# Clustered attention and a gated MLP: key tiles in float32, a pair taken head by head, and a new order of work

## The chip, the cores and the metric

The kernel runs on one core of one Trainium2 chip. The core has five engines that run side by side, each through its own queue in order: TensorE (PE) multiplies matrices, VectorE (DVE), ScalarE (ACT) and GpSimd (POOL) work on tiles, and SyncE (SP) issues transfers. The metric is the device time of one execution in microseconds; less is better.

## The reference

Four batches, eight heads, 768 positions, 64 columns a head, 16 clusters. Everything is float32. Cut to what is computed:

```python
# attention, for each batch and head
q_assign = argmax(normalized(q) @ normalized(centroids).T)
k_assign = argmax(normalized(k) @ normalized(centroids).T)
scores = where(q_assign[:, None] == k_assign[None, :], q @ k.T / 8, -1e9)
attn = softmax(scores)
out = attn @ v
# the heads side by side give x: [4, 768, 512]
h = relu(x @ w_in)                 # [4, 768, 1024]
u, v = h[..., :512], h[..., 512:]
v_n = (v - mean(v)) / sqrt(var(v) + 1e-6)
v_s = einsum('ts,bsd->btd', w_spatial, v_n) + b_spatial[None, :, None]
result = (u * v_s) @ w_out
```

## The kernel before

The kernel works on pairs of heads: four pairs make a batch, sixteen the whole. Products that must keep float32 accuracy are made of float16 parts: a tile is written as a high part (a cast on ACT) and a low part (what the cast left over), and three products of parts are summed in PSUM. A row of the profile names the tile without its number.

A pair goes through three functions. `prep(n)` loads k and q (`raw`) and v (`vraw`), makes high parts (`hq`, L616) and low parts (`lo`, L622 on DVE, or L619 and L620 on ACT and POOL for the pairs in `LO_POOL`), multiplies with the centroids (L638 to L640), finds each position's cluster by five DVE operations (L651 to L656) and puts the one-hot rows into `hq` (L686 for pair 0, transposing transfers for the others). It also makes the parts of v (`vhl`, L690 and L695, or L692 and L693 for the pairs in `VL_POOL`) and v's sums over all keys (by PE for the pairs in `SUM_PE`, L703 and L704; else by a DVE reduction, L711, and one small float32 product, L712). `shifts(n)` finds each query's largest score: products L754 on PE, maxima L761 on DVE (18 instructions a pair, over 24 products), and brings the result as extra rows into `hq` (L774 to L793). `attend(n)` makes the scores (L823 and L825: 24 products of 512 columns and 24 of 256 a pair), the exponentials on ACT (L830, 18 a pair, into the float32 tiles `p`), and for each of 12 key tiles a pair (six a head) a cast on ACT (L842), a subtraction on POOL (L846) and 18 products with the values on PE (L852: for each of six query blocks high by high, high by low, low by high, each with 65 or 64 moving columns; 228 a pair with those that add the mean).

`mlp(b)` follows a batch, in groups of six products of 512 columns (all at L900): first v (with mean and variance on DVE, L928 and L929, a chain of small operations for the inverse root, L934 to L939, of which the power, L935, is on POOL, and the normalization L941 on DVE), then u, the product with w_spatial (L900 `vn`, `wsp`) with the gating L964 to L966, a transposing transfer (`gT`), and the product with w_out.

The order of the instructions is made by a planner in the kernel: every operation has a cost, a due time and a key, and whenever an engine comes free in the plan's own time, the ready operation with the least due time plus key is written next on it. Engines then run their queues in that order. Attention and MLP work are interleaved on PE in this way, so that the MLP's long products fill in where a pair's scores or values are not ready.

Of the kernel before, what the change touches and what calls it, by code (L numbers as in the profile page):

```python
# [7 lines left out]
F32 = mybir.dt.float32  # L8
# [69 lines left out]
KC = -44.31  # L78
# [45 lines left out]
SHIFT = {}  # L124
# [66 lines left out]
class Plan:  # L191


    def __init__(self):
        self.ops = []
        self.rings = []
        self.due = None
        self.tag = ""
# [6 lines left out]
    def op(self, eng, cost, fn, after=(), use=(), new=(), claim=(), key=0.0, at=0.0, dma=None, turn=False, cols=0, alt=None, due=None, port=None):  # L205
# [4 lines left out]
        o.key = key + SHIFT.get(o.tag, 0.0) if key < FILLER else key  # L210
        o.eng, o.cost, o.fn, o.key, o.at, o.dma, o.turn, o.cols, o.alt = eng, cost, fn, key, at, dma, turn, cols, alt
# [127 lines left out]
def kernel(  # L339
# [43 lines left out]
    ohx = const.tile([P, NT, 8, C], F16, name="ohx")  # L383
    shx = [const.tile([P, NT, P], F16, name="shx%d" % i) for i in range(1)]
# [17 lines left out]
    held = {"wou": wou}  # L402

# [36 lines left out]
    r_vhl = R(None, "vhl", None, None, V_BUFS, tiles=vhl)  # L440
    scratch = r_p32.new()
# [15 lines left out]

    ld_c = op("SP", 0.6, lambda: nc.sync.dma_start(out=cn(0), in_=cent), new=[scratch], dma=0.1, key=KC)
    ld_i = op("SP", 0.6, lambda: nc.sync.dma_start(out=idt(), in_=ident), use=[scratch], dma=0.2, key=KC)
# [7 lines left out]
    c_wt = op("DVE", 1.2, fill, key=-8)  # L467
    c_id = op("DVE", 0.2, lambda: V.tensor_copy(out=id16, in_=idt()), after=[ld_i], use=[scratch], key=0)
    c_z = op("DVE", 0.5, lambda: (V.memset(cmh, 0.0), V.memset(cml, 0.0)), key=-8)
    c_oh = op("POOL", 1.0, lambda: (G_.memset(ohx, 0.0), G_.memset(ohx.rearrange("p t (x e) c -> p t x (e c)", e=2)[:, :, 0:2, C:C + 1], PEN)), key=-8)  # L470
    c_sh = op("POOL", 2.0, lambda: [G_.memset(x, 0.0) for x in shx], key=-7)
    c_mean = op("POOL", 0.6, lambda: [G_.memset(x, 0.0) for x in mean], key=-6)
    c_wh = op("POOL", 0.5, lambda: (G_.memset(one32, 1.0), [G_.memset(x[:, :, D:D + 1], S * MEAN_UNIT) for x in whs], [G_.memset(x[:, :, D:D + 1], 0.0) for x in wls]), key=-5)
    c_one = op("POOL", 0.8, lambda: [G_.memset(x[:, :, :, D:D + 1], 1.0) for x in vhl], key=-9)
# [11 lines left out]
        (0.25, lambda: V.tensor_scalar(out=cn(0), in0=cn(0), scalar1=ninv, scalar2=C_SCALE, op0=ALU.mult, op1=ALU.mult)),  # L486
        (0.22, lambda: V.tensor_copy(out=cn(1), in_=cn(0))),
# [560 lines left out]
```

## Time and profile before

| what | us |
|---|---|
| median of three runs | 665.71 |
| lowest, highest | 665.3, 668.3 |
| span of the profiled execution | 666.4 |

The profiled execution's own time is not listed apart from the three; its span lies among them, 0.7 us above the median. Busy time is an engine's share of the span in which at least one of its instructions ran. A matmul's duration on PE holds its way through the array, which the next matmul overlaps: the pace is read from start to start, not from the duration. Idle time of an engine costs something only where another engine waits for it.

### The profile page before, as it was taken

To read this page: it belongs to the slowest core of one execution; us is meant where nothing else is said; L and a number is where in the kernel's file an instruction comes from. 1 tells how busy PE (TensorE), PEld (TensorE's weight loads), DVE (VectorE), ACT (ScalarE), POOL (GpSimd) and SP (SyncE) were. 2 spreads that over 40 slices of the span, in tenths; PEclk is the share of its full clock that TensorE was granted. 3 is DMA by queue.
4 is the path that set the end of the run, shared out by engine and by line. 5 is a ranking of instruction groups with operands and counts; after the bars stand their busy time and mean duration, and the time that the engine had idled before them with its cause. 6 is when DMAs were issued, how large, how long until landed. Compare 5 with 4: busy or idle time off the path is not lost.

```text
span 666.4 us, 16687 instructions
## 1 busy us (share of the span) xinstructions
PE 624.9 (94%) x6757; PEld 374.9 (56%) x6757; DVE 446.3 (67%) x828; ACT 454.6 (68%) x875; POOL 426.5 (64%) x305
## 2 busy tenths in 40 slices
PE   1799988889999999989999999999999999999996
PEld 1466665556556665656666465566665564444442
DVE  5899989999999979966969756764378210142100
ACT  6489998998879796869876596259984761232211
POOL 3268997988877886677796486149996681132210
PEclk9999998999999999989999999999999999999999
DMA  5656876684733785787434616133023203220124
GB/s 171 156 118 137 174 168 176 153 194 74 161 97 73 165 169 157 168 157 164 133 73 92 157 44 135 35 83 60 9 59 53 60 10 56 54 64 32 32 63 95
DMA packets 105939, 70.49 MB, mean 106 GB/s; under 512 B 90315, under 2 KB 93062, under 8 KB 105862
## 3 DMA queue, kind: packets, MB, share of 16 engines
q1 hardware_dynamic: 102118, 62.74, 43.1%
q10 hardware_dynamic: 3744, 6.69, 2.8%
q8 instruction: 53, 0.87, 0.5%
q14 instruction: 24, 0.20, 0.1%
HBM read 27.63 MB, written 6.29 MB: 51 GB/s over the span
## 4 chain that ended last, share of the span: by engine, by line
PE 66%; DVE 16%; DMA 8%; ACT 7%; issue 2%; SPq 0%; POOL 0%; POOLq 0%; DVEq 0%; ACTq 0%
PE acc L900 36%; PE acc L852 11%; PE acc L823 6%; PE acc L825 6%; DVE nm L761 6%; PE acc L754 5%; DMA gT<-ghl 2%; ACT pt L842 2%; ACT p L830 2%; DVE lo L622 2%; DMA vraw<-in_vp_dram 1%; DMA raw<-in_kqT_dram 1%; DMA wraw<-in_wsT_dram 1%; DMA sht<-shx 1%; DMA hq<-sht 1%
## 5 line engine op out<-in xcount | busy, mean ns | idle before, releaser
L846 POOL TENSOR_TENSOR pt<-p,pt 128x768 f16<-128x768 f32 x192 | 319.9, 1692 | 60.6 <-ACT pt L842 39.9
L761 DVE TENSOR_REDUCE nm<-acc 128x1 f32<-128x512 f32 (+1 forms) x288 | 185.6, 678 | 28.8 <-PE acc L754 27.4
L830 ACT ACTIVATE p<-acc 128x512 f32<-128x512 f32 x288 | 156.3, 598 | 25.0 <-PE acc L825 20.8
L842 ACT CAST pt<-p 128x768 f16<-128x768 f32 x192 | 152.2, 835 | 2.0
L852 PEld LDWEIGHTS <-pt 128*128 128x128 f16 x3456 | 129.0, 98 | 33.2 <-POOL pt L846 4.4
L852 PE MATMUL acc<-vhl,pt 128*128 128x65 f16 (+1 forms) x3456 | 138.4, 193 | 3.1 <-POOL pt L846 2.8
L900 PE MATMUL acc<-win,xT 128*128 128x512 f16 x576 | 137.9, 379 | 0.2
L823 PE MATMUL acc<-hq,lo 128*128 128x256 f16 (+1 forms) x384 | 111.0, 330 | 5.4 <-ACT p L830 4.5
L825 PE MATMUL acc<-hq 81*128 81x256 f16 (+1 forms) x384 | 111.2, 330 | 1.8 <-DMA hq<-sht 1.7
L900 PE MATMUL acc<-vn,wsp 128*128 128x512 f16 x432 | 102.1, 379 | 0.0
L754 PE MATMUL acc<-hq 80*128 80x256 f16 (+1 forms) x384 | 92.9, 339 | 3.8 <-DVE nm L761 1.5
L966 POOL TENSOR_TENSOR ghl<-u,ghl 128x512 f16<-128x512 f32 x24 | 28.5, 1188 | 100.6 <-ACT ghl L965 89.1
L900 PEld LDWEIGHTS <-xT 128*128 128x128 f16 x576 | 55.3, 97 | 62.4 <-issue 2.1
L964 DVE SCALAR_TENSOR_TENSOR u<-acc,bsp,u 128x512 f32<-128x512 f32 x24 | 18.0, 749 | 84.6 <-PE acc L900 84.5
L900 PE MATMUL acc<-wou,gT 128*128 128x512 f16 x288 | 70.1, 383 | 2.3 <-DMA gT<-ghl 2.3
L900 PEld LDWEIGHTS <-wsp 128*128 128x128 f16 x432 | 41.4, 97 | 45.8 <-issue 0.2
L965 ACT CAST ghl<-u 128x512 f16<-128x512 f32 x24 | 14.8, 617 | 61.5 <-DMA gT<-ghl 36.2
L823 PEld LDWEIGHTS <-lo 128*128 128x128 f16 x384 | 35.6, 98 | 31.5 <-issue 9.0
L754 PEld LDWEIGHTS <-hq 80*128 80x128 f16 x384 | 34.9, 100 | 24.9 <-issue 4.5
L825 PEld LDWEIGHTS <-hq 81*128 81x128 f16 x384 | 37.8, 98 | 18.0 <-issue 6.3
L900 PEld LDWEIGHTS <-gT 128*128 128x128 f16 x288 | 28.1, 98 | 34.7 <-DMA gT<-ghl 3.0
L943 POOL TENSOR_TENSOR vn<-v,vn 128x512 f16<-128x512 f32 x24 | 28.8, 1219 | 19.3 <-ACT vn L942 19.3
(108 smaller groups left out, 642.7 us busy)
## 6 DMA issues: line engine op xcount, KB each, us to landing
raw<-in_kqT_dram SPq DMA_DIRECT2D x15, 768.0 KB
vraw<-in_vp_dram SPq DMA_DIRECT2D x16, 384.0 KB
out_dram<-o ACTq DMA_DIRECT2D x24, 256.0 KB
hq<-hq SPq DMA_DIRECT2D x15, 384.0 KB
vn<-in_w_in_dram SPq DMA_DIRECT2D x8, 512.0 KB
hq<-lo SPq DMA_DIRECT2D x16, 192.0 KB
lo<-hq SPq DMA_DIRECT2D x16, 192.0 KB
wraw<-in_wsT_dram SPq DMA_DIRECT2D x12, 192.0 KB
```

The lines of the kernel that those rows point to most:

```text
L754: T.matmul(out=acc.t[:, c:c + cs.stop - cs.start], lhsT=hq.t[0:R_SH, 1, h, t * P:(t + 1) * P], rhs=hq.t[0:R_SH, 0, h, cs], start=c == 0, s ...
L761: V.tensor_reduce(out=nm.t[:, t, k:k + 1] if n == 1 else nm.t[:, t:t + n, k], in_=src, axis=AX.X, op=ALU.max, negate=True)
L823: T.matmul(out=o, lhsT=lo.t[:, h, ks], rhs=hq.t[:, 2, h, cs], start=x == 0, stop=False, skip_group_check=True)
L825: T.matmul(out=o, lhsT=hq.t[0:R_E, 0, h, ks], rhs=hq.t[0:R_E, 1, h, cs], start=False, stop=True, skip_group_check=True)
L830: o = op("ACT", 0.6, lambda: A.activation(out=p32.t[:, j0:j0 + n_, cs], in_=sc.t.rearrange("p (t c) -> p t c", t=n_), func=AF.Exp, bias=P_ ...
L842: o = op("ACT", 0.83, lambda pt=pt, p32t=p32t: A.copy(out=pt.t[:, 0, :], in_=p32t()), after=[done[k % 2], done[2]], use=[p32], new=[pt], k ...
L846: los_.append(op("POOL", 1.64 if SPLIT == 1 else 0.09 + 1.64 / SPLIT, lambda pt=pt, p32t=p32t, qs=qs: G_.tensor_tensor(out=pt.t[:, 1, qs], ...
L852: T.matmul(out=av.t[:, t * (D + 1):t * (D + 1) + w], lhsT=lhsT, rhs=rhs, skip_group_check=True, **f)
L900: T.matmul(out=acc.t, lhsT=lr[m][0], rhs=lr[m][1], start=(m == 0), stop=(m == n - 1))
L943: l = op("POOL", 1.16, lambda t=t, v=v: G_.tensor_tensor(out=vn[:, 1, t, :], in0=v.t, in1=vn[:, 0, t, :], op=ALU.subtract), after=[h], use ...
L964: o = op("DVE", 0.75, lambda: V.scalar_tensor_tensor(out=u32.t, in0=acc.t, scalar=bsp[:, t:t + 1], in1=u32.t, op0=ALU.add, op1=ALU.mult), ...
L966: l = op("POOL", 1.16, lambda: G_.tensor_tensor(out=ghl.t[:, 1, :], in0=u32.t, in1=ghl.t[:, 0, :], op=ALU.subtract), after=[h], use=[u32, ...
```

## The change

- **Key tiles in float32.** In the four pairs of the first batch, two of six key tiles of each head (`WHOLE`, tiles 1 and 4) no longer get a cast and a subtraction. Their exponentials meet the values as float32: six products a tile of 65 columns in place of 18 float16 ones. The float32 values (`vf`) lie in the space of the weight tile `wou`, whose loads therefore wait until the last such product; an ACT operation writes them.
- **Low parts moved to GpSimd.** `LO_POOL` takes pairs 2 and 3 as well, `VL_POOL` pairs 2, 3 and 4. The sums of v of pairs 4 to 7 go from DVE to PE.
- **Pair 0 head by head.** `prep0` makes high parts, logits, clusters, one-hot rows and their transposes for one head and then the other, in pieces; the centroids' parts are written by ACT and DVE; `shifts(0)` brings head 0's result in two parts (four key tiles, then two).
- **The inverse root in the MLP.** Its small operations move from DVE to POOL, and in batch 0 ACT normalizes in place of DVE.
- **Order from a table.** `STARTS` holds a rank for each operation; the rank takes the place of due time and key.

```diff
+WHOLE = {0: [(0, 1), (0, 4), (1, 1), (1, 4)], 1: [(0, 1), (0, 4), (1, 1), (1, 4)], 2: [(0, 1), (0, 4), (1, 1), (1, 4)], 3: [(0, 1), (0, 4), (1, 1), (1, 4)]}
-LO_POOL = (1,)
-VL_POOL = (0, 1)
-SUM_PE = tuple(range(4))
+LO_POOL = (1, 2, 3)
+VL_POOL = (0, 1, 2, 3, 4)
+SUM_PE = (0, 1, 2, 3, 4, 5, 6, 7)
+C_TINY = 0.25
+NORM_ACT = (0,)
...
+        if self.starts is not None and key < FILLER:
+            o.due, o.key = float(self.starts[len(self.ops)]), 0.0
...
+    wouf = wou.rearrange("p a t f -> p (a t f)").bitcast(F32)
+    vw = NT * 2 * (D + 2)
+    vfs = [wouf[:, vw * i:vw * (i + 1)].rearrange("p (t h d) -> p t h d", h=2, d=D + 2) for i in range(VF_BUFS)] if WHOLE else []
...
+            o = o_vs = op("ACT", 0.83, lambda: A.activation(out=full(), in_=vraw.t.rearrange("p t (h d) -> p t h d", d=D), func=AF.Copy, scale=V_SCALE), after=[o_vh, c_one], use=[vraw], new=[vf] if vf else [], key=KV)
+            if n in VL_POOL:
+                o_vl = op("POOL", 1.59, lambda: G_.tensor_tensor(out=vh.t[:, :, :, D + 2:], in0=full(), in1=vh.t[:, :, :, 0:D], op=ALU.subtract), after=[o], use=[vf or vraw, vh], key=KV)
...
+    def prep0():
...
+        for h in range(2):
+            kh = h * K0_HEAD
...
+            lg = op("PE", 0.35, logits, at=A0_H1 * h, after=[hi, low] + c_cm, use=[hq, lo], new=[misc], cols=576, key=K0_LG + kh)
...
+            o = op("DVE", 0.35, lambda lgf=lgf, mx=mx: V.tensor_reduce(out=mx.t[:, 0:NA], in_=lgf(), axis=AX.X, op=ALU.max), after=[lg], use=[misc], new=[mx], key=KA)
...
+                    rows[z].append(op(("DVE", "ACT")[a], (0.62, 0.37)[z], copy, after=[trs[z], lg, qa], use=[hq, tp[z]], key=K0_ROW + kh))
...
+            for z, (t0, t1) in enumerate(((0, 4), (4, NT)) if fast else ((0, NT),)):
...
-                o = op("ACT", 0.83, lambda pt=pt, p32t=p32t: A.copy(out=pt.t[:, 0, :], in_=p32t()), after=[done[k % 2], done[2]], use=[p32], new=[pt], key=K_HI)
+                got = [done[k % 2], done[2]]
+                if not whole:
+                    fast = (h, k) in CAST_V.get(n, ())
+                    o = op("DVE" if fast else "ACT", C_CAST if fast else 0.83, lambda pt=pt, p32t=p32t, fast=fast: (V.tensor_copy if fast else A.copy)(out=pt.t[:, 0, :], in_=p32t()), after=got, use=[p32], new=[pt], key=K_HI, port=fast)
+                    o = op("POOL", 1.64, lambda pt=pt, p32t=p32t: G_.tensor_tensor(out=pt.t[:, 1, :], in0=p32t(), in1=pt.t[:, 0, :], op=ALU.subtract), after=[o], use=[p32, pt], key=K_LO)
+                    got = [o]
...
+                        if whole:
+                            mm(t, D + 1, p32t()[:, ts], X["vf"].t[:, k, h, 0:D + 1], start=False, stop=stop)
+                            continue
...
-            o = op("DVE", 0.2, lambda: V.tensor_scalar(out=a.t, in0=mv.t[:, :, 1], scalar1=1e-6, scalar2=None, op0=ALU.add), after=ags, use=[mv], new=[a], key=0, port=True)
+            o = op("POOL", C_TINY, lambda: G_.tensor_scalar(out=a.t, in0=mv.t[:, :, 1], scalar1=1e-6, scalar2=None, op0=ALU.add), after=ags, use=[mv], new=[a], key=-2)
...
+                if b in NORM_ACT:
+                    o = op("ACT", 0.72, lambda k=k, v=v: A.activation(out=v.t, in_=v.t, func=AF.Identity, scale=y.t[:, k:k + 1], bias=y2.t[:, k:k + 1]), after=[yb], use=[v, y, y2], key=T_NRM)
...
+    for o in w_ops["wou"]:
+        o.after += vf_users
```

On DVE, in the head of the program, the maxima of pair 0's first head (`nm`) stand like this before, up to the reduction `nl` that ends them; `acc_111` holds pair 1's logits, and `w` belongs to v's sums:

```order
L654 TENSOR_TENSOR acc_111<-acc_111,wt 128x384
L761 TENSOR_REDUCE nm_86<-acc_106 128x1
L655 TENSOR_REDUCE m_350<-acc_111 128x24
L721 SCALAR_TENSOR_TENSOR w_353<-acc_108,wh_89 2x2x65
L656 TENSOR_TENSOR acc_111<-acc_111,m_350 128x384
L761 TENSOR_REDUCE nm_86<-acc_109 128x1
L761 TENSOR_REDUCE nm_86<-acc_110 128x2
L761 TENSOR_REDUCE nm_86<-acc_107 128x1
L761 TENSOR_REDUCE nm_86<-acc_112 128x1
L761 TENSOR_REDUCE nm_86<-acc_105 128x2
L761 TENSOR_REDUCE nm_87<-acc_106 128x1
L774 TENSOR_REDUCE nl<-nm_86 128x6
```

And like this with the change, from pair 0's one-hot rows (`hq`, the first two of head 0, the others of head 1) to the first `nl`:

```order
L789 CAST hq<-acc_109 17x512
L789 CAST hq<-acc_110 17x256
L789 CAST hq<-acc_111 17x512
L923 TENSOR_REDUCE nm_87<-acc_112 128x1
L789 CAST hq<-acc_113 17x256
L923 TENSOR_REDUCE nm_87<-acc_106 128x2
L923 TENSOR_REDUCE nm_87<-acc_107 128x1
L923 TENSOR_REDUCE nm_87<-acc_108 128x1
L923 TENSOR_REDUCE nm_87<-acc_112 128x2
L923 TENSOR_REDUCE nm_87<-acc_106 128x1
L923 TENSOR_REDUCE nm_87<-acc_110 128x1
L941 TENSOR_REDUCE nl<-nm_87 128x4
```

Seven maxima now stand ahead of the first `nl`, which covers four key tiles, in place of ten ahead of one that covers six; pair 1's logits have moved behind it.

On PE, at pair 0's second key tile, this is one query block of the values before:

```order
L852 LDWEIGHTS pt
L852 MATMUL acc_107<-vhl_84,pt 128x65
L852 LDWEIGHTS pt
L852 MATMUL acc_107<-vhl_84,pt 128x64
L852 LDWEIGHTS pt
L852 MATMUL acc_107<-vhl_84,pt 128x65
```

And this is the end of the first key tile and all of the second with the change (a float32 product has no weight load of its own in this listing; `wou` is the space that holds the float32 values):

```order
L1025 LDWEIGHTS pt
L1025 MATMUL acc_109<-vhl_85,pt 128x65
L916 LDWEIGHTS hq
L916 MATMUL acc_106<-hq 128x512
L1025 MATMUL acc_109<-wou,p_403 128x65 x6
```

Eighteen loads and products of a key tile have become six products that read `p` itself.

On POOL, at the second inverse root of the first MLP, before (`y<-a,mhalf` is the power, `pt` the subtractions of the key tiles):

```order
L846 TENSOR_TENSOR pt<-p_3317,pt 128x768 x2
L935 TENSOR_TENSOR y<-a,mhalf 128x2
L846 TENSOR_TENSOR pt<-p_3375,pt 128x768 x2
L943 TENSOR_TENSOR vn<-v_3304,vn 128x512
L943 TENSOR_TENSOR vn<-v_3327,vn 128x512
```

And with the change:

```order
L1112 TENSOR_SCALAR a<-mv 128x2
L1113 TENSOR_TENSOR y<-a,mhalf 128x2
L1020 TENSOR_TENSOR pt<-p_3223,pt 128x768 x2
L1114 TENSOR_TENSOR y_3402<-y 128x2
L1056 TENSOR_TENSOR xhl<-xn,xhl 128x6x64
L1115 TENSOR_TENSOR y_3402<-y_3402,a 128x2
L1020 TENSOR_TENSOR pt<-p_3356,pt 128x768
L1116 TENSOR_SCALAR y_3402<-y_3402 128x2
L1020 TENSOR_TENSOR pt<-p_3356,pt 128x768
L1117 TENSOR_TENSOR y<-y,y_3402 128x2
```

The small steps of the root now stand between long subtractions on one queue. On PE, 114 of the MLP's products stand ahead of pair 8's first score with the change and 204 before, and 30 more of the products for the maxima stand ahead of it.

## Rows read from the trace of the kernel before

**Rows 1.** The page: busy time and instructions of PE; its busy tenths in 40 slices.

```profile
PE 624.9 (94%) x6757; PEld 374.9 (56%) x6757; DVE 446.3 (67%) x828; ACT 454.6 (68%) x875; POOL 426.5 (64%) x305
PE   1799988889999999989999999999999999999996
```

**Rows 2.** Busy time by stretch: PE, PEld, DVE, ACT, POOL; granted clock, DMA share, GB/s.

```profile
0.00:32.20 32.20, 14.25 (x130) 8.89 (x131) 21.95 (x70) 17.73 (x30) 9.96 (x21) 1.00 0.59 167
32.20:264.40 232.20, 218.15 (x2931) 143.64 (x2930) 217.78 (x384) 203.47 (x403) 191.41 (x123) 0.99 0.62 143
264.40:666.40 402.00, 392.49 (x3699) 222.34 (x3697) 206.58 (x376) 233.41 (x443) 225.17 (x161) 0.99 0.37 79
```

**Rows 3.** The same stretches, products of the MLP (L900) alone: PE, PEld.

```profile
32.20:264.40 232.20, 49.12 (x204) 19.59 (x204) 0.99 0.62 143
```

**Rows 4.** PE in order of time: start, duration, instructions; pair 0's first score, paces, pair 8's.

```profile
32.21 0.63 PE L823 MATMUL acc<-hq,lo 128*128 128x512 f16 x1
...
39.85 0.71 PE L852 MATMUL acc<-vhl,pt 128*128 128x65 f16 x18
40.40 0.38 PE L823 MATMUL acc<-hq,lo 128*128 128x512 f16 x1
...
101.11 0.38 PE L712 MATMUL acc<-vs,one 128*2 128x128 f32 x2 [2.18 <-DVE nm L761]
...
264.37 0.38 PE L823 MATMUL acc<-hq,lo 128*128 128x512 f16 x1
```

**Rows 5.** The chain that ended last, in order of time: start, length, what.

```profile
38.05 0.03 PE acc L638
...
51.00 3.80 DMA sht<-shx
...
279.88 5.29 DMA gT<-ghl
...
546.17 103.61 PE acc L900 x480
```

**Rows 6.** Groups by line and form: count, busy us, mean ns of one, idle before.

```profile
L846 POOL TENSOR_TENSOR pt<-p,pt 128x768 f16<-128x768 f32 x192 | 319.9, 1692 | 60.6 <-ACT pt L842 39.9 <-issue 15.1 <-PE acc L825 2.3
L842 ACT CAST pt<-p 128x768 f16<-128x768 f32 x192 | 152.2, 835 | 2.0
L852 PEld LDWEIGHTS <-pt 128*128 128x128 f16 x3456 | 129.0, 98 | 33.2 <-POOL pt L846 4.4 <-issue 3.3 <-ACT shx L778 0.3
L622 DVE SCALAR_TENSOR_TENSOR lo<-raw,hq 128x768 f16<-128x768 f32 x30 | 36.2, 1207 | 0.4 <-ACT hq L616 0.2
L878 POOL TENSOR_TENSOR xhl<-xn,xhl 128x384 f16<-128x384 f32 x32 | 33.4, 1045 | 11.8 <-PE acc L900 5.3 <-ACT xhl L877 5.2 <-PE acc L825 0.8
L695 DVE SCALAR_TENSOR_TENSOR vhl<-vraw,vhl 128x768 f16<-128x768 f32 x14 | 19.2, 1371 | 0.6 <-ACT vhl L690 0.6
L711 DVE TENSOR_REDUCE vs<-vraw 128x128 f32<-128x768 f32 x12 | 18.0, 1503 | 8.3 <-DMA vraw<-in_vp_dram 8.3
L941 DVE TENSOR_SCALAR v<-v,mv,y 128x512 f32<-128x512 f32 x24 | 15.9, 705 | 0.2
L490 PEld LDWEIGHTS acc<-p 128*128 128x128 f32 x1 | 0.2, 180 | 10.1 <-DVE p L487 10.1
```

**Rows 7.** DVE in the head, in order of time: pair 0's clusters, rows and first maxima.

```profile
15.41 0.57 DVE L656 TENSOR_TENSOR acc<-acc,m 128x384 f32<-128x384 f32 x1
17.45 1.01 DVE L686 CAST hq<-acc 17x512 f16<-17x512 f32 x2 [1.48 <-ACT raw L619]
...
19.83 0.69 DVE L761 TENSOR_REDUCE nm<-acc 128x1 f32<-128x512 f32 x1
...
26.07 3.66 DVE L761 TENSOR_REDUCE nm<-acc 128x1 f32<-128x512 f32 x6
29.65 0.15 DVE L774 TENSOR_REDUCE nl<-nm 128x6 f32<-128x18 f32 x1
```

**Rows 8.** DVE in order of time at the first inverse root of the MLP.

```profile
206.55 0.16 DVE L936 TENSOR_TENSOR y<-y 128x2 f32<-128x2 f32 x1
...
207.22 1.08 DVE L937 TENSOR_TENSOR y<-y,a 128x2 f32<-128x2 f32 x1
```

More of the change, by code (lines that the diff above doesn't have):

```diff
@@ L77 @@
 KP0 = -109.76
-KC = -44.31
+K0_HI = -155.0
+K0_LO = -100.0
+K0_QA = -105.0
+K0_QB = -60.0
+K0_LG = -130.0
+K0_AM = -130.0
+K0_TP = -130.0
+K0_ROW = -130.0
+K0_MX = -110.0
+K0_MAX = -110.0
+K0_SH = -120.0
+K0_HEAD = 20.0
+SHIFT_PE = (0,)
+A0_H1 = 0.0
+D0_ATT = (-40.0, -20.0)
+A0_SV = 17.0
+LO0_POOL = False
+WHOLE = {0: [(0, 1), (0, 4), (1, 1), (1, 4)], 1: [(0, 1), (0, 4), (1, 1), (1, 4)], 2: [(0, 1), (0, 4), (1, 1), (1, 4)], 3: [(0, 1), (0, 4), (1, 1), (1, 4)]}
+CAST_V = {}
+C_F32 = 1.0
+C_CAST = 0.58
+VF_BUFS = 2
+LO_STT = ()
+KC = -144.31
+KC0 = -160.0
+KC1 = -150.0
+K_FILL = -8.0
 T_LO = 10.12
@@ L713, in prep @@
         else:
-            o = op("PE", 0.75, sums, after=[o_vh, o_vl, c_wt], use=[vh], new=[sv], cols=1548, key=KS)
+            o = op("PE", 0.75, sums, at=0.0 if n else A0_SV, after=[o_vh, o_vl, c_wt], use=[vh], new=[sv], cols=1548, key=KS)
         wh, w32, wl = r_wh.new(), r_w32.new(), r_wl.new()
@@ L746, in shifts, with ready @@
             tops = []
+            n_ = n
+            def ready(parts, h=h):
+                if n_:
+                    return X["rows"][h]
+                rows, qa = X["rows"][h]
+                got = [qa]
+                for t, cs, c in parts:
+                    got += [rows[cs.start // 512][0], rows[t * P // 512][1]]
+                return got
             def top(parts, col, n, h=h, nm=nm, tops=tops):
@@ L754, in scores @@
                         T.matmul(out=acc.t[:, c:c + cs.stop - cs.start], lhsT=hq.t[0:R_SH, 1, h, t * P:(t + 1) * P], rhs=hq.t[0:R_SH, 0, h, cs], start=c == 0, stop=c > 0 or n == 1, skip_group_check=True)
-                o = op("PE", 0.2155, scores, after=X["rows"][h] + maxed[-MX_AHEAD:][:1], use=[hq], new=[acc], cols=512, key=K_MX)
+                o = op("PE", 0.2155, scores, after=ready(parts) + maxed[-MX_AHEAD:][:1], use=[hq], new=[acc], cols=512, key=K0_MX + K0_HEAD * h if n_ == 0 else K_MX)
                 def most():
@@ L779, in shifts @@
-            if n == 0 and h == 0:
-                tp = [r_acc.new() for _ in parts]
-                tr = op("PE", 0.4, lambda sx=sx, tp=tp: spread(tp, lambda t: sx.t[:, t, :]), after=cols + [c_id], use=[sx], new=tp, cols=S, key=K_SH)
-                def add(tp=tp, h=h):
-                    for a, cs in zip(tp, parts):
-                        d = hq.t[R_OH:R_END, 1, h, cs]
-                        V.tensor_tensor(out=d, in0=a.t[R_OH:R_END, 0:cs.stop - cs.start], in1=d, op=ALU.add)
-                X["shift"].append(op("DVE", 1.05, add, after=[tr], use=[hq] + tp, key=K_SH))
+            fast = n == 0 and h in SHIFT_PE
@@ L796, in attend @@
+            X["shift"][h].append(sp(lambda sht=sht, h=h: nc.sync.dma_start(out=hq.t[R_SH:R_END, 1, h, :], in_=sht.t[R_SH:R_END].rearrange("c t s -> c (t s)")), 0.1, after=[tr], use=[hq, sht], key=KS))
     def attend(n):
```

391 lines of the change are left out of this document (255 added, 136 removed).

## Prediction

> **What bounds the kernel now.** I read the page first, then the stretches, then PE in order of time. PE is busy 94% of the span [rows 1], and its slices show where the rest is: the first two slices, small holes up to 200 us, and the end. But a busy PE is not a PE at its pace, so I counted work. The pure MLP stretch at the end repeats a product of 512 columns every 103.61/480 = 0.216 us [rows 5]; one of 256 is taken as half. Eighteen value products start at 39.85 and the next group at 40.40 [rows 4]: 0.0306 us each. A small logit product adds about 0.03 [rows 5].
>
> Three stretches follow from two events: pair 0's first score at 32.21 and pair 8's at 264.37 [rows 4]. In the middle one, 232.2 us long, PE's work by count is: scores of eight pairs at 24 x 0.216 + 24 x 0.108 = 7.8, together 62; 214 products for maxima at 0.162 less the few of the head, 33; 1824 values, 56; 288 logits, 8; 204 MLP products [rows 3], 44. That is 203, and 29 us are missing. In the same stretch DVE is busy 217.8, ACT 203.5 and POOL 191.4 of 232.2 [rows 2]: DVE sets the pace at 94%, with ACT close behind, and the MLP's products are too few to cover it. In the last stretch DVE and ACT are busy about half of 402 us and PE 392.5: PE's own work bounds it. So a gain can come from the head and from the middle, and whatever the change adds to PE's work costs its full price unless it falls into the 29 us.
>
> **The head.** Pair 0's five cluster operations end at 15.98, the first maximum starts at 19.83, the reduction that closes head 0 at 29.65 [rows 7], the first score at 32.21. With the change each operation has half the columns: ten of about 0.35 us (an estimate between half of 0.57 and all of it), eight of them ahead of head 0's result, 2.8 us as the five now: no gain there. Now a wait of 1.5 for ACT and two pairs of copies, 1.01 each [rows 7], with a second wait between, stand ahead of the first maximum; with the change it is one pair and a half, 1.6 us, begun near 16.0 because the transposes no longer wait behind pair 1's scalings on ACT: the first maximum starts near 17.8, 2.0 gained. Then seven maxima at 3.66/6 = 0.61 and one small copy, 4.6 us, in place of 9.8 us in which pair 1's logits stood between [rows 7]: 5.2 gained. What follows the reduction is the same chain, 2.5 us. First score: 17.8 + 4.6 + 2.5, about 25.0; gain 7.2.
>
> **The float32 key tiles.** Sixteen tiles lose a cast of 835 ns on ACT and a subtraction of 1692 ns on POOL [rows 6]: 13 and 27 us. On PE, 18 products (0.55 us) become six in float32. No such product stands in the trace; the nearest show two records each: the pair of L712 takes 0.38 with one record 0.27 long, so two records of 128 columns start 0.11 apart [rows 4]. For 65 columns that is 0.055, twelve records 0.66 us a tile: the lower bound, if loads hide. A float32 weight load of 128 columns takes 180 ns against 98 for float16 [rows 6], and float16 loads repeat every 0.031 with their products: 0.031 + 0.082 = 0.113 a load, twelve 1.35 us. With loads laid bare it is 12 x 0.18 = 2.16, the upper bound. I take 1.35, because the load's row is for the same 128 columns: +0.8 a tile, +12.8 us of PE in all (bounds +1.8 and +25.8). The Trainium skill, "TensorE: Matmul & The Clock Gate", section "Weight-path perf modes — Fast Weight Load (FWL) and DoubleRow", says that the fast weight load is not used for float32, and its section "LDWEIGHTS (loading the stationary operand)" gives 128/1.2 = 107 ns a load; by that, an estimate, the tile costs 1.28 us and the extra is 11.7 in place of 12.8. The rows agree as far as they go, 180 against 98.
>
> **Work moved off DVE.** In the middle stretch DVE loses four low parts at 1.21 and three of v at 1.37, four sums of v at 1.50, six normalizations at 0.71 [rows 6], three roots of some 2.7 us (an estimate: two of the five steps take 0.16 and 1.08 [rows 8]), and four gatings behind S, at a normalization's price, that the new order puts behind pair 8: 30 us. It gains 22 maxima ahead at 0.61, 13 us, and 5 us of pair 1 and head 1 that the earlier first score leaves behind it. DVE: 217.8 - 30 + 18 = 206. ACT: 203.5 - 13 for casts, + 6 for seven scalings at a cast's price, + 4 for normalizing, - 3 for MLP tiles put off, + 2 from the head: 199. POOL: 191.4 - 27, + 11 for seven low parts at some 1.6, - 5 for MLP tiles put off, and 21 small steps. A small step on POOL is in no row; the two sizes of its subtraction (1045 ns for 384 columns, 1692 for 768 [rows 6]) leave 0.4 us at no columns. Bounds: nothing, and 1.05, the 384-column row; I take 0.4 because the steps have two columns: POOL 179 (170 to 192), under the others at either end.
>
> The long second of the two steps in [rows 8] shows why this move can be worth more than its count: the same tiny size took 0.16 and 1.08 us on DVE. The Trainium skill, "SBUF — State Buffer", section "Who interferes with whom", says that a DVE instruction with two SBUF inputs and a GpSimd one that reads SBUF block each other for the whole instruction; the rows agree, and the sum does without it.
>
> **PE at pair 8.** Against before, the new order has by then 90 MLP products fewer (-19.4), 30 for maxima more (+4.9), 36 logits more (+1), 48 for sums of v for five small ones (+1.5), 72 values not done yet (-2.2), and the float32 extra (+12.8): -1.3. So PE has done the same work, 202, and what counts is when. With DVE 206, PE 202 and ACT 199 nothing lies far behind. At 94% the stretch is 219; at 100%, 206. I take 214, 96%: POOL's load falls, and with it the blocking, but three engines are now equal, so a wait of any one counts.
>
> **The rest** has the 402 us of now, and all PE work that the change adds and that is not done by pair 8: 12.8 + 1.5 + 1.3 = 15.6. I take off 2 of the one long wait there (5.29 us for `gT` [rows 5]), since the products with w_out now stand further behind the S products that feed them. That is 416. The last three tiles stand as before; `wou`'s loads wait for pair 3's values, and the first product with w_out stands among the last scores of pair 9: nothing.
>
> **Sum.** 25 + 214 + 416 = 655, against the span of 666.4. The median lies 0.7 below that span: 654.
>
> **Rivals.**
> 1. *Float32 tiles dear.* Loads laid bare, 2.16 us. PE then has 215 in the middle, which at 96% is 224; 25 + 224 + 416 = 665. For it speaks that PE is near the others already; against it that float16 loads hide. 0.10.
> 2. *Latency sets the middle.* The 29 us are waits for transfers, such as 3.80 us for `sht` [rows 5], and stay. 202 + 29 = 231, less some 5 where float32 work fills a hole: 226; sum 667. The DMA share of 0.62 [rows 2] speaks for it, DVE's 94% against it. 0.12.
> 3. *GpSimd's queue delays the MLP: slower.* The root's steps stand between subtractions; two of them between steps add 3.4 us, and S waits for all six tiles. Twelve chains; hidden while other PE work stands in between. From five that show, 655 + 17 = 672, and seven give 679. 0.11.
> 4. *All three engines pack.* The middle takes 206 and the rest 414: 645. 0.15.
> The forecast has 0.52.
>
> **How the numbers follow.** What a measurement of this kernel can tell from no change is 0.5%, 3.3 us: 662.4 to 669.0. Faster: most of the forecast (0.48), all of rival 4 (0.15), a little of 1 and 2 (0.05): 0.68. Slower: rival 3 (0.10) and the tails of 1 and 2 (0.03): 0.13. Same: 0.19. Range: 645 (rival 4) to 668 (rivals 1 and 2); beyond lie rival 3 and the tails.
>
> **What would show it.** Pair 0's first score near 25; pair 8's near 239, with 114 MLP products ahead of it; DVE busy about 206 in between; a float32 tile of 1.2 to 1.4 us on PE between neighbours; the last stretch within 5 us of 416. Wrong if the first score comes after 29, if a float32 tile takes over 2 us, or if PE waits for `vn` in front of S.

## The result, and the profile after

The changed kernel takes 653.95 us (median of four runs, 653.64 to 654.37); the kernel before took 665.5 beside it (665.06 to 668.3). The recorded ratio is 0.9833 (the two medians alone give 0.9827), with a 95% interval from 0.9801 to 0.9864: faster by 1.7%, clear of the 0.5% that the prediction took as the least that can be told. The profiled execution spans 652.4 us. Two executions behind the table of experiments were slow (809.4 us of `t_bare`, the profiled one, and 678.9 of `t_moves`); the ratios leave them out, and `t_bare` has no trace that can be compared.

The page, as in [rows 1]: PE's busy share, its slices, and the granted clock by slice.

```profile
span 652.4 us, 16639 instructions
PE 626.1 (96%) x6707; PEld 387.5 (59%) x6707; DVE 405.1 (62%) x754; ACT 449.1 (69%) x879; POOL 428.2 (66%) x366
PE   2799999999999999999999999999999999999996
PEclk9989999999999999999999999999999999999999
```

DVE's busy time fell from 446.3 to 405.1 us and the holes in PE's early slices are gone. The stretches between the same two events as in [rows 2] (pair 0's first score, now at 23.00, and pair 8's, now at 239.6); columns: PE, PEld, DVE, ACT, POOL, granted clock, DMA share, GB/s.

```profile
0.00:23.00 23.00, 10.49 (x126) 7.50 (x127) 16.16 (x63) 14.89 (x28) 10.25 (x25) 1.00 0.64 175
23.00:239.60 216.60, 208.71 (x2789) 151.05 (x2787) 203.22 (x371) 192.95 (x398) 171.22 (x127) 0.99 0.70 154
239.60:652.40 412.80, 406.95 (x3797) 228.92 (x3795) 185.73 (x322) 241.27 (x454) 246.72 (x214) 1.00 0.36 81
```

The head takes 9.2 us less, the middle 15.6 less, and the rest 10.8 more: together 14.0 less, the difference of the two spans. The medians differ by only 11.6. Wherever the record has both, an execution's time lies 1.7 to 2.2 us above its span, so the span of 666.4 belongs to the execution of 668.3, the slowest of the kernel before; some 2.5 of the 14.0 us are that execution's own. The MLP's products alone in the middle stretch, as in [rows 3]:

```profile
23.00:239.60 216.60, 27.22 (x114) 10.81 (x114) 0.99 0.70 154
```

For the experiments I counted PE's work pair by pair from its records: a product at its columns at the upper clock level (2.4 GHz) plus 2.5 ns, which gives the 0.216 for 512 columns of [rows 5], and a float32 value product at 1.34/12 us. The 2.5 ns are what 103.61/480 us of [rows 5] leaves over 512 columns at that level. What a stretch is longer than this sum is "missing": waits of PE and time at the lower clock. Before and after, from one pair's first score to the next one's (the rest ends with PE's last product, 3.5 to 3.8 us before the span does):

```
pair                0     1     2     3     4     5     6     7   middle   rest (pairs 8 to 15)
before  start    32.2  55.7  79.7 107.5 133.1 160.1 196.0 232.9
        missing   5.4   3.5   8.1   6.3   4.7   3.3   1.8   1.0    34.1    14.8
        work     18.1  20.5  19.7  19.3  22.3  32.7  35.1  30.5   198.2   383.3
after   start    23.0  55.0  79.5 104.1 129.9 155.8 183.0 212.4
        missing   8.6   0.8   1.5   1.3   1.7   1.2   0.7   2.1    17.9     9.8
        work     23.4  23.8  23.0  24.6  24.2  26.0  28.6  25.0   198.6   399.5
```

PE's work up to pair 8 is the same (198.2 and 198.6); 16 of its missing 34 us are gone. That is the gain of the middle, and it had to pay for the float32 tiles first. PE's records show only 14.0 of the 34.1 us as idle, and 7.9 of the 17.9: the other part is short waits under overlapping records, the lower clock, and logit products, which repeat every 0.025 us and are counted at 0.016 (some 3 us in each middle). The prediction counted from paces, with 0.03 for a logit product, and so had 203 and 29 where this count has 198.2 and 34.1.

### The profile page after: what moved, and what is told of

Its sections match the earlier page's. It is cut to its first block, busy times and chain, and to the rows that moved or that the text cites. A ratio compares the mean times of both kernels' runs of the same rounds, so it can differ in the third digit from the quotient of the medians.

```text
span 652.4 us, 16639 instructions
## 1 busy us (share of the span) xinstructions
PE 626.1 (96%) x6707; PEld 387.5 (59%) x6707; DVE 405.1 (62%) x754; ACT 449.1 (69%) x879; POOL 428.2 (66%) x366
## 4 chain that ended last, share of the span: by engine, by line
PE 73%; DVE 3%; DMA 2%; ACT 2%; POOL 2%; issue 1%; POOLq 0%; ACTq 0%; DVEq 0%; SPq 0%
PE acc L1078 39%; PE acc L1025 13%; PE acc L997 7%; PE acc L999 7%; PE acc L916 6%; DMA gT<-ghl 2%; DVE nm L923 2%; POOL pt L1020 1%; ACT pt L1019 1%; ACT p L1004 1%; POOL ghl L1150 1%; DVE wsp L619 1%; DVE lo L821 0%; DMA wraw<-in_wsT_dram 0%; PE acc L835 0%
## 5 line engine op out<-in xcount | busy, mean ns | idle before, releaser
L1020 POOL TENSOR_TENSOR pt<-p,pt 128x768 f16<-128x768 f32 x176 | 296.8, 1703 | 77.2 <-ACT pt L1019 62.8
L1004 ACT ACTIVATE p<-acc 128x512 f32<-128x512 f32 x288 | 159.3, 600 | 45.4 <-PE acc L999 24.9
L1019 ACT CAST pt<-p 128x768 f16<-128x768 f32 x176 | 143.5, 839 | 18.0 <-PE acc L1025 17.0
L1078 PE MATMUL acc<-win,xT 128*128 128x512 f16 x576 | 134.9, 379 | 0.3 <-DVE nm L923 0.3
L1025 PEld LDWEIGHTS <-pt 128*128 128x128 f16 x3168 | 114.0, 97 | 19.6 <-POOL pt L1020 1.5
L1025 PE MATMUL acc<-vhl,pt 128*128 128x65 f16 (+1 forms) x3168 | 121.1, 193 | 1.2 <-POOL pt L1020 1.1
L916 PE MATMUL acc<-hq 80*128 80x256 f16 (+1 forms) x384 | 98.4, 330 | 3.2 <-DMA hq<-oht 1.1
L1078 PE MATMUL acc<-vn,wsp 128*128 128x512 f16 x432 | 99.1, 379 | 0.2 <-ACT p L1004 0.2
L1078 PE MATMUL acc<-wou,gT 128*128 128x512 f16 x288 | 68.2, 379 | 1.7 <-DMA gT<-ghl 1.7
L1148 DVE SCALAR_TENSOR_TENSOR u<-acc,bsp,u 128x512 f32<-128x512 f32 x24 | 17.9, 747 | 83.2 <-PE acc L1078 81.5
L999 PEld LDWEIGHTS <-hq 81*128 81x128 f16 x384 | 37.5, 98 | 18.1 <-issue 1.9
L1149 ACT CAST ghl<-u 128x512 f16<-128x512 f32 x24 | 14.8, 617 | 34.6 <-DMA gT<-ghl 23.2
L1159 ACT ACTIVATE o<-acc 128x512 f32<-128x512 f32 x24 | 14.3, 597 | 34.0 <-PE acc L1078 30.6
```

The costliest lines, as they stand in the source:

```text
L916: T.matmul(out=acc.t[:, c:c + cs.stop - cs.start], lhsT=hq.t[0:R_SH, 1, h, t * P:(t + 1) * P], rhs=hq.t[0:R_SH, 0, h, cs], start=c == 0, s ...
L999: T.matmul(out=o, lhsT=hq.t[0:R_E, 0, h, ks], rhs=hq.t[0:R_E, 1, h, cs], start=False, stop=True, skip_group_check=True)
L1004: o = op("ACT", 0.6, lambda: A.activation(out=p32.t[:, j0:j0 + n_, cs], in_=sc.t.rearrange("p (t c) -> p t c", t=n_), func=AF.Exp, bias=P_ ...
L1019: o = op("DVE" if fast else "ACT", C_CAST if fast else 0.83, lambda pt=pt, p32t=p32t, fast=fast: (V.tensor_copy if fast else A.copy)(out=p ...
L1020: o = op("POOL", 1.64, lambda pt=pt, p32t=p32t: G_.tensor_tensor(out=pt.t[:, 1, :], in0=p32t(), in1=pt.t[:, 0, :], op=ALU.subtract), after ...
L1025: T.matmul(out=av.t[:, t * (D + 1):t * (D + 1) + w], lhsT=lhsT, rhs=rhs, skip_group_check=True, **f)
```

## Experiments

Each version is given by its ratio to the kernel before on the same chip, with the 95% interval; the kernel before stood there between 663.0 and 664.7 us (665.5 for the change itself).

```
version      head  moves  tiles  order       median   ratio   interval           pair 1  pair 8  missing, pairs 0-3, 4-7
the change   new   yes    4      table       653.95   0.9833  0.9801 to 0.9864     55.0   239.6   12.2   5.7
head_only    new   no     0      keys        684.91   1.0295  1.0256 to 1.0335     73.1   279.6   44.0  20.4
head_f32     new   no     4      keys        702.93   1.0574  1.0535 to 1.0613     83.7   294.6   38.0  28.3
head_moves   new   yes    0      keys        671.77   1.0107  1.0077 to 1.0138     61.2   259.1   34.0  15.2
all_keys     new   yes    4      keys        672.27   1.0113  1.0078 to 1.0149     64.9   256.8   21.4  16.3
t_bare       new   no     0      table       678.4    1.0220  1.0177 to 1.0263
t_f32        new   no     4      table       677.52   1.0214  1.0176 to 1.0253     56.5   259.7   14.4  26.5
t_moves      new   yes    0      table       665.05   1.0024  0.9999 to 1.0049     57.3   247.3   30.3   9.1
t_f32x6      new   yes    6      table       658.79   0.9945  0.9917 to 0.9973     55.0   243.1    8.0   6.8
b_relief     old   yes    4      old keys    679.87   1.0205  1.0152 to 1.0257     63.8   265.8   20.6  15.8
t_late0      new   yes    4      table       662.96   0.9961  0.9935 to 0.9986     59.8   248.8   13.7   9.7
t_lg2        new   yes    4      table       665.12   1.0000  0.9972 to 1.0028     58.6   249.3   15.3  11.3
q_lg2        new   yes    4      written out 654.25   0.9858  0.9826 to 0.9890     54.9   240.2   12.6   5.9
```

"Moves" are the low parts, sums of v, roots and normalizations together; "tiles" is how many of a pair's twelve key tiles stay float32 in the first four pairs. `t_bare` is told by its times alone.

**The parts without the table.** `STARTS` is emptied, so the planner goes by due times and keys; then parts are undone.

```diff
-STARTS = (
...
-)
+STARTS = ""
-WHOLE = {0: [(0, 1), (0, 4), (1, 1), (1, 4)], 1: [(0, 1), (0, 4), (1, 1), (1, 4)], 2: [(0, 1), (0, 4), (1, 1), (1, 4)], 3: [(0, 1), (0, 4), (1, 1), (1, 4)]}
+WHOLE = {}
-LO_POOL = (1, 2, 3)
-VL_POOL = (0, 1, 2, 3, 4)
-SUM_PE = (0, 1, 2, 3, 4, 5, 6, 7)
-NORM_ACT = (0,)
+LO_POOL = (1,)
+VL_POOL = (0, 1)
+SUM_PE = tuple(range(4))
+NORM_ACT = ()
-            o = op("POOL", C_TINY, lambda: G_.tensor_tensor(out=y2.t, in0=y.t, in1=y.t, op=ALU.mult), after=[o], use=[y], new=[y2], key=-2)
+            o = op("DVE", 0.18, lambda: V.tensor_tensor(out=y2.t, in0=y.t, in1=y.t, op=ALU.mult), after=[o], use=[y], new=[y2], key=0, port=True)
...
```

Head alone (all of the above undone):

> The kernel before with pair 0 taken head by head and nothing else of the change: no float32 tile, low parts, sums of v, roots and normalizations where they were, order from keys and due times. Theory 1 (relief): the middle stretch is set by DVE, ACT and POOL, so the head's 7 us come through only in part: first score near 23 to 25, pair 8's near 262, 661 us. Theory 2 (the table): the parts are worth little without the new order, and every version whose order comes from keys lies between 661 and 666: this one 663. Theory 3 (the head is all): 7 to 9 us come through and this version is near 657.

Head and tiles (`WHOLE` kept):

> Head by head, and the sixteen float32 tiles; the moves off DVE and the table left out. PE has 12.8 us more work, ACT 13 less, POOL 27 less, DVE as before. Theory 1: DVE still sets the middle, so the tiles bring little by themselves: the casts and subtractions were not last. 661 against 661 of the head alone, with the 12.8 us on PE hidden in the holes of the first four pairs. Theory 2: 663. A rival to both (PE's work is dear): the extra 12.8 us show in full, near 670.

Head and moves (only `WHOLE` emptied):

> Head by head, and the moves (low parts and sums of v, roots on GpSimd, normalizations of the first batch on ACT), without float32 tiles and without the table. DVE loses 17 us or more in the middle, POOL gains some 15 and ACT some 10. Theory 1: ACT and POOL, now near 210, take DVE's place, and the middle does not get shorter: 660. Theory 2: 663. If DVE alone was the bound, the middle shortens by 10 and the kernel is near 652.

All but the table (only `STARTS` emptied):

> The whole change except the table of ranks: the order comes from keys and due times. It has the same 114 MLP products ahead of pair 8's first score as the change has. Theory 1: relief of all three engines is the gain, and the table moves only some work about: pair 8 near 242, 656 us. Theory 2: the table is most of the gain: 662 to 665.

All three theories missed: none of the four lies between 655 and 666, and the new head with keys loses 21 us, with the tiles 39. The head does start early (first score at 24.4 in `head_only`), but pair 1's first score comes at 73.1 in place of 55.7. In between the engines stand for transfers. One wait each on PE, ACT and DVE of `head_only`, in order of time (start, duration, instructions, idle time before and what ended it):

```profile
36.72 0.51 PE L979 MATMUL acc<-mean,hq 83*128 83x65 f16 x6 [5.35 <-DMA mean<-wl]
```

```profile
43.77 1.58 ACT L769 ACTIVATE hq<-raw 128x768 f16<-128x768 f32 x2 [3.70 <-DMA raw<-in_kqT_dram]
```

```profile
36.21 0.55 DVE L806 TENSOR_TENSOR acc<-acc,m 128x384 f32<-128x384 f32 x1
44.77 0.17 DVE L604 TENSOR_SCALAR bsp<-bsp 128x6 f32<-128x6 f32 x1 [8.01 <-DMA bsp<-in_b_sp_dram]
44.85 0.96 DVE L775 SCALAR_TENSOR_TENSOR lo<-raw,hq 128x768 f16<-128x768 f32 x1
```

DVE's 8.0 us are put down to the load of the MLP's bias, an operation without hurry that stands in its queue; but the low part behind it needs the high part that ACT starts at 43.77, so the wait would have been nearly as long without the bias. What they have in common is that SP issues late. The issues of pair 0's means, pair 1's one-hot transpose and the next k and q, first of `head_only`, then of the change:

```profile
34.03 1.32 SPq L671 DMA_DIRECT2D mean<-wl  x2
...
37.56 0.57 SPq L765 DMA_DIRECT2D raw<-in_kqT_dram  x1
38.23 1.25 SPq L819 DMA_TRANSPOSE oht<-ohx  x1
```

```profile
26.55 0.56 SPq L717 DMA_DIRECT2D mean<-wl  x1
27.26 1.34 SPq L865 DMA_TRANSPOSE oht<-ohx  x1
...
34.52 0.57 SPq L811 DMA_DIRECT2D raw<-in_kqT_dram  x1
```

The same transfers go out 3 to 11 us earlier in the change, because work that feeds them comes earlier: DVE begins pair 1's clusters at 21.03 in the change, ahead of most maxima of pair 0's second head, and at 29.77 in `head_only`, behind them. With the whole change the keys reach 672.27: the table is worth 18 us beside it, and ten of them are there by pair 1 (first score 1.9 us later, then 40.0 us for pair 0 against 32.0).

**The parts with the table.** Ranks stay with their operations: one that the table does not know takes a rank just behind what it reads, and the rank of one that is gone is passed over. The diffs are as above without the first.

Neither moves nor tiles:

> The changed kernel with its table of ranks and its head, without float32 tiles and with all moved work back where it was (casts and subtractions that the table does not know take a rank between their exps and their products). Same 114 MLP products ahead of pair 8. Theory 1 (relief): DVE near 218 and POOL near 191 in the middle set its length again: about 225 there, 664 in all. Theory 2 (the table): the order alone makes the gain, and without the 14 us of extra PE work the kernel is even faster than the change: 645 to 652.

Tiles without moves:

> Table, head and float32 tiles; low parts, sums of v, roots and normalizations back where they were. Theory 1: casts and subtractions are gone from ACT and POOL in the first four pairs, DVE is the only full engine: 660. Theory 2: no dependence on the moves, 654.

Moves without tiles:

> Table, head and moves, without float32 tiles: 13 us more on ACT, 27 more on POOL, 12.8 less on PE. Theory 1: the holes of pairs 0 to 3 come back, some 12 us there, against 12.8 us less work on PE later: about 656 to 660. Theory 2: float32 tiles only cost, so 642 to 645.

Two tiles more (six of twelve):

```diff
+WHOLE = {n: [(h, k) for h in range(2) for k in (1, 2, 4)] for n in range(4)}
```

> The change with six of twelve key tiles in float32 in place of four: 6.4 us more on PE, 6.7 less on ACT, 13.5 less on POOL. Theory 1: PE misses only some 2 us in each of pairs 1 to 3, so further relief finds nothing to fill: 658 to 660. If relief still pays there, 651.

The table alone is no gain either, so theory 2 falls: `t_bare` and `t_f32` are 2% slower than the kernel before. Without the moves the tiles bring nothing (1.0220 and 1.0214); with them they bring 1.9 points (1.0024 and 0.9833). These steps are not the worth of the parts alone. The ranks were made for the whole change, and the planner remakes the order around what is put back: lined up group by group in the first eight pairs, about half of PE's order in `t_moves` and two thirds in `t_f32` match the change's, against nine tenths in `t_lg2` (below), which lost 11 us by its new order alone. How much of each step is relief and how much is order is not shown. Where the time differs is in what is missing. From `t_moves` to the change, pairs 0 to 3 lose 18.1 us of holes (30.3 to 12.2) and take 12.8 us more PE work (82.0 to 94.8). From `t_f32` to the change it is pairs 4 to 7: 26.5 to 5.7. There DVE is full in `t_f32`, and the granted clock is below 1.00. First the busy time in pairs 5 and 6 (PE, PEld, DVE, ACT, POOL; then the granted clock), then DVE's groups there (count, busy us, mean ns):

```profile
158.70:231.20 72.50, 63.76 (x740) 39.77 (x737) 71.22 (x121) 55.05 (x110) 52.02 (x34) 0.92 0.48 107
```

```profile
L1137 DVE TENSOR_SCALAR v<-v,mv,y 128x512 f32<-128x512 f32 x4 | 5.4, 1350 | 0.0
...
L1128 DVE TENSOR_TENSOR y<-y,y 128x2 f32<-128x2 f32 x2 | 2.6, 1304 | 0.0
L1126 DVE TENSOR_TENSOR y<-y,a 128x2 f32<-128x2 f32 x2 | 2.6, 1284 | 0.0
```

DVE is busy 71.2 of 72.5 us, and products on two columns take 1.3 us, as the long one of [rows 8] did. Six such products fall into this stretch. One takes 0.14 us, with nothing on GpSimd beside it; the other five take 1.01 to 1.60 us, and each ends within 0.02 us of the end of a subtraction on GpSimd. The Trainium skill, "SBUF — State Buffer", section "Who interferes with whom", has the rule for this: a DVE instruction with two SBUF inputs contends with a GpSimd one that reads SBUF. These five agree. The normalization takes 1350 ns where the mean before was 705 [rows 6]; it has one tile and scalars as inputs, so that rule does not name it. That the moves take such operations out of DVE's way may be why they seem worth more than their number; no run separates it. The change's own pairs 5 and 6, same columns:

```profile
155.80:212.40 56.60, 56.26 (x742) 37.81 (x741) 55.03 (x96) 53.19 (x109) 53.15 (x47) 1.00 0.64 139
```

Six tiles in place of four cost 7 us by the ratios (6.6 in the spans), a little more than the 4 to 6 of theory 1: pairs 0 to 3 have 6.5 us more work and only 4.2 less missing, and the rest of the kernel misses 3.0 more, which I cannot assign.

**Relief in the old order.** The kernel before, with `LO_POOL`, `VL_POOL`, `SUM_PE`, `NORM_ACT`, the roots and `WHOLE` of the change; head, keys and due times its own.

```diff
-LO_POOL = (1,)
-VL_POOL = (0, 1)
-SUM_PE = tuple(range(4))
+LO_POOL = (1, 2, 3)
+VL_POOL = (0, 1, 2, 3, 4)
+SUM_PE = (0, 1, 2, 3, 4, 5, 6, 7)
+NORM_ACT = (0,)
+WHOLE = {0: [(0, 1), (0, 4), (1, 1), (1, 4)], 1: [(0, 1), (0, 4), (1, 1), (1, 4)], 2: [(0, 1), (0, 4), (1, 1), (1, 4)], 3: [(0, 1), (0, 4), (1, 1), (1, 4)]}
...
```

> The kernel before, with its own head and its own keys and due times, plus the float32 tiles and all the moves: no head by head, no table. 126 MLP products stand ahead of pair 8's first score (before: 204). If relief of the three engines is a gain by itself, whatever the order, the first eight pairs shorten by some 15 us against 14 us of extra PE work later that was hidden in holes: 655 to 660. If the parts only pay together with an order made for them, it is no faster than before: 664 to 672, with holes of 5 us and more in pairs 4 to 7.

It is 2% slower: the second outcome, and somewhat worse than its range. Its middle stretch (PE, PEld, DVE, ACT, POOL; then the granted clock):

```profile
34.10:265.80 231.70, 219.13 (x2761) 154.07 (x2759) 193.30 (x343) 197.05 (x393) 172.29 (x129) 0.94 0.61 143
```

DVE, ACT and POOL are relieved as planned (217.8, 203.5 and 191.4 before [rows 2]), none is busy much over 85%, and the stretch is as long as before: 231.7 against 232.2. The lower clock has a part in it (0.94 here, 0.99 before), but not the whole: the fastest of the four executions, at a mean granted clock of 0.997 in place of 0.976, still took 674.95. So relief alone, in the old order, is no gain. No engine is full in this version; PE's waits there are spread over many causes, the largest 2.2 us in all, and none of them was tested alone.

**The head's lead, and one hole.** Pair 1 starts at 55.0 after a lead of 9.2 us at pair 0, against 55.7. The first version delays pair 0's scores; the second moves pair 2's logits behind two score units of pair 0, since PE waits there and the granted clock falls behind it; the third does the same with every engine's order held fast.

```diff
...
+                X["nl%d" % h] = o
...
-after=X["go"][h] + [X["shift"]
+after=X["go"][h] + ([X["nl1"]] if n == 0 else []) + [X["shift"]
...
```

> The changed kernel, but pair 0's scores also wait for the reduction that closes head 1's maxima (31.97 in the changed kernel's profile), so that its first score comes near 32, as in the kernel before. If the head's lead counts in full, as the prediction's sum has it (7.2 us of 11), the kernel loses 7 to 9 us: 661 to 663. If the lead is used up inside pair 0 anyway (pair 1's first score stood at 55.0 in the changed kernel against 55.7 before), it loses 0 to 2: 654 to 656, with pair 1's first score near 55 to 57.

```diff
-        lg = op("PE", 0.92, logits, after=
+        lg = op("PE", 0.92, logits, at=36.0 if n == 2 else 0.0, after=
...
```

> The changed kernel with pair 2's logits placed some 2 us later in PE's order, behind two scores and the first value products of pair 0: in the changed kernel they stand at 31.3, wait 1.49 us for a low part, and the granted clock then reads 0.50 for some 3.4 us. If this hole and the slow stretch behind it set pair 1's start, 1.5 to 3 us are gained: 651 to 652.5, with no slice at 0.50 between 32 and 40. If pair 1's preparation sets it, the time stays at 654.

```diff
...
                 for o in q:
+                    if o.seq != queue[e][0]:
+                        continue
                     g = gate(o)
...
```

> The changed kernel with every engine's order of work written down and kept, and in PE's order one thing moved: pair 2's logits stand behind the next two score units of pair 0 instead of ahead of them. Nothing else in any engine's order differs. If the 11 us that the earlier attempt at this lost came from the order further down, which the planner had made anew, this version is at 654 or below: 651 to 652.5 if the hole of 1.49 us and the slow stretch behind it set pair 1's start, 654 if pair 1's preparation sets it. If the placement itself costs (the logits are late for pair 2, or the scores wait longer than the logits did), it is at 657 or above, with pair 1's first score after 57.

`t_lg2` lost 11 us, which no theory had. With the order held fast the same move costs nothing (654.25, ratio 0.9858 beside 0.9833), so the loss came from what the planner made of all that follows: one operation 2 us later in the plan, and the picks after it differ as far as pair 7, with 2.8 and 5.7 us missing in pairs 3 and 4 in place of 1.3 and 1.7. The move itself does not gain either. PE's windows of the change, with PE busy and granted clock:

```profile
32.00:33.00 1.00, 0.20 (x8) 1.00 0.65 123
33.00:34.00 1.00, 1.00 (x32) 0.69 0.14 40
34.00:35.00 1.00, 1.00 (x5) 0.50 0.65 130
35.00:36.00 1.00, 1.00 (x16) 0.50 1.59 168
36.00:37.00 1.00, 1.00 (x18) 0.60 0.57 99
```

The clock is at its lower level (1.2 GHz) from 33.4 to 36.8, behind the wait that ends at 32.8. In `q_lg2` that wait is gone; three of its four executions show a mean granted clock of 1.000 (the change's four show 0.994 to 0.996), and the time stays. In its profiled execution the clock is low for twice as long (27.7 to 34.5), and pair 1 still starts at 54.9. The last wait of PE ahead of pair 1's first score is the same in both, for pair 2's one-hot rows (`hq<-oht`, 1.1 us in the change and 0.8 in `q_lg2`). So neither the hole nor the lower clock sets pair 1's start. What stands last in front of it is pair 2's preparation, for some 1 us; when pair 1's own would have let it start was not tested.

`t_late0` came out at 662.96, the number of its first outcome (the lead counts in full). But its first score is at 29.1 and not near 32, and `t_lg2`, with a first score only 1.5 us later than the change's, lost more; both stand in an order that the planner made anew, so this loss is no measure of the lead. The two can be compared with each other, as they have nearly the same order from pair 1 on. Their first scores are at 29.1 and 24.5, at pair 1 they are at 59.8 and 58.6, at pair 8 at 248.8 and 249.3. Of a lead of 4.6 us at pair 0, 1.2 are left at pair 1 and nothing at pair 8. For the change against the kernel before this is not shown in full: pair 1's first score is only 0.7 us earlier, but PE has by then done 4.3 us more work (29.0 in place of 24.8, counted as above), so some 5 of the 9.2 us are still there.

No version tried beats the change.

## Why the prediction held, step by step

**The sum.** 25 + 214 + 416 was predicted, 23.0 + 216.6 + 412.8 is measured, so the terms are off by 2 to 3 us each and cancel in part: a span of 655 was forecast, 652.4 is measured. The median of 654 came out at 653.95, and that it is so near is luck. The last step took 0.7 off the span, because the span before lay 0.7 above its median. That span belongs to the slowest of the three executions, as shown above; an execution's time is about 2 us more than its span, and the changed kernel's median lies 1.6 above the profiled span. This error of 2.3 us makes up for the 2.6 that the sum was too long.

**The head.** The first score came 2.0 earlier than worked out. From the first maximum on the working holds: 5.0 us from there to the reduction (4.6), 2.24 on to the score (2.5). DVE's rows of the change, in order of time:

```profile
9.87 0.36 DVE L764 TENSOR_REDUCE mx<-acc 128x12 f32<-128x192 f32 x1 [0.69 <-PE acc L753]
...
14.12 1.61 DVE L789 CAST hq<-acc 17x512 f16<-17x512 f32 x3 [1.25 <-ACT hq L789]
15.77 0.69 DVE L923 TENSOR_REDUCE nm<-acc 128x1 f32<-128x512 f32 x1
...
20.76 0.16 DVE L941 TENSOR_REDUCE nl<-nm 128x4 f32<-128x12 f32 x1
```

The ten smaller cluster operations take 0.35 to 0.37, as estimated. What I left out lies ahead of them: the centroids and the first high parts come earlier too, so the first cluster operation starts at 9.87 (13.02 before). I also left out the wait of 1.25 us for ACT that still stands in front of the copies; the two errors partly cancel. The sum counts the lead in full, and that step is in doubt: between `t_late0` and `t_lg2` a lead of 4.6 us was gone by pair 8, and of the change's own 9.2 us some 4 are lost by pair 1.

**The float32 tile.** 1.35 us was taken, between 0.66 and 2.16. PE in order of time (start, duration, instructions):

```profile
36.92 1.45 PE L1025 MATMUL acc<-wou,p 128*128 128x65 f32 x12
38.21 0.81 PE L916 MATMUL acc<-hq 80*128 80x256 f16 x4
...
49.81 1.53 PE L1025 MATMUL acc<-wou,p 128*128 128x65 f32 x12
51.18 0.38 PE L997 MATMUL acc<-hq,lo 128*128 128x256 f16 x2
```

From its first record to the next product it is 1.29 us behind a long product and 1.37 behind a value product; over all sixteen the mean is 1.32, the extra work 12.3 us (predicted 12.8). Rival 1 falls. The rule of the Trainium skill cited there ("TensorE: Matmul & The Clock Gate", section "LDWEIGHTS (loading the stationary operand)", 107 ns a load; by estimate 1.28 us a tile) is as near as my row.

**Work moved off DVE.** DVE 203.2 us in the middle (206), ACT 193.0 (199), POOL 171.2 (179). The small steps on POOL, of which no row stood before, took 196 to 408 ns on the mean (0.4 assumed), the power 704; groups by form:

```profile
L1113 POOL TENSOR_TENSOR y<-a,mhalf 128x2 f32<-128x2 f32 x12 | 8.4, 704 | 0.8
L1114 POOL TENSOR_TENSOR y<-y 128x2 f32<-128x2 f32 x12 | 4.5, 372 | 0.6
...
L1117 POOL TENSOR_TENSOR y<-y,y 128x2 f32<-128x2 f32 x12 | 2.4, 196 | 0.8
```

**PE at pair 8.** 114 MLP products ahead, and equal work: +0.4 in place of -1.3. The share of 96% is the term that was too good: the stretch came out at 216.6 with DVE busy 203.2 of it, the same 94% as before. And its reason was too short. I took the new order to move MLP products and the relief to fill the holes. `b_relief` has all of the relief and none of the gain; `all_keys` has it with the new head, 18 us short. The likely reading is that the relief makes the room and the table's order uses it: no version that lacked the table, the moves or the tiles was faster than the kernel before. How much each gives is not shown, since every version that leaves a part out was also planned anew.

**The rest.** 412.8 against 416: the added work is there (383.3 to 399.5, +16.2 for 15.6 predicted), and I took 2.0 off for waits where 5.0 went (14.8 to 9.8 missing). The wait that I took them off is mostly not where they went: the 5.29 us for `gT` [rows 5] are the transfer's own time on the chain, and PE waited 2.3 us for it before and 1.7 after. PE's waits for `gT` behind pair 0's first score, before and after (us in total, times, longest):

```profile
PE acc L900 <- DMA gT<-ghl: 2.3, 1, 2.3
```

```profile
PE acc L1078 <- DMA gT<-ghl: 1.7, 1, 1.7
```

**The other rivals.** No row of PE's waits names `vn`, so rival 3 falls, although its interleaving is there on POOL: two subtractions stand between two steps of the first root.

```profile
152.51 0.72 POOL L1113 TENSOR_TENSOR y<-a,mhalf 128x2 f32<-128x2 f32 x1
153.19 3.25 POOL L1020 TENSOR_TENSOR pt<-p,pt 128x768 f16<-128x768 f32 x2
156.41 0.91 POOL L1114 TENSOR_TENSOR y<-y 128x2 f32<-128x2 f32 x1
```

Rival 4 (206 for the middle) needed no waits at all; 17.9 us of them are left, half in pair 0. Rival 2 (late inputs set the middle) was wrong for the change. In `b_relief` its 231 us before the discount come back as 231.7, but by other terms: 195.2 of work and 36.4 missing, in place of 202 and 29, part of it the lower clock, and only 0.5 us of PE's named waits there end with a transfer. What spoke against the rival was DVE's 94%, and a busy DVE does not rule out that something else is late once DVE is relieved.

What stays open: how much of the table's 18 us is undone damage of the new head's keys and how much is gain over a well-kept order by keys, since neither the old head with the table nor newly set keys were tried; how fast the versions without moves or without tiles would be with a table made for each of them; and by which of its many places the table gains.

## What to carry to other kernels

Here several engines were nearly full, and taking work off them showed no gain in an order that was not made for it; test such parts together and one by one, and count what PE misses pair by pair, since the busy share hides it. With a planner that picks greedily, one operation placed 2 us later remade the picks behind it and cost 11 us here: to test a place, or the worth of a part, hold every engine's order fast and move that one thing. Where a start is made earlier, look at the transfers of the next tile on the issuing queue: here they went out up to 11 us later where the early work stood in front of what feeds them.

## What the runs showed of the hardware that was not expected

A float32 product of 65 columns comes as two records whose starts lie 0.11 us apart, at a granted clock of 1.00 (twelve in 1.29 to 1.37 us), though a load's own record lasts 0.19:

```profile
L1025 PEld LDWEIGHTS acc<-wou,p x192: 187/192/268, 36.6 to 129.7; 128*128 128x128 f32 x192
```

The granted clock is not a function of the order alone: in the profile of `q_lg2` it falls at 27.7 us, behind the same products and the same waits (1.32 and 0.52 us) after which it stays at 1.00 in the change's profile, and in three other executions of `q_lg2` its mean is 1.000. Two slices of that profile (PE busy, then the granted clock):

```profile
27.00:28.00 1.00, 0.40 (x2) 0.85 0.00 0
28.00:29.00 1.00, 0.54 (x3) 0.50 0.23 45
```
